# Attention and two feed-forward layers on one core: the table of attention's steps in a new order

## The chip, the core and the metric

One core of a Trainium2 chip runs the whole program: one launch, inputs and outputs in HBM. The time is device microseconds of one execution, the median of the runs shown. The engines are TensorE (PE, with its weight loads apart as PEld), VectorE (DVE), ScalarE (ACT), GpSimd (POOL) and SyncE (SP), which here only issues DMAs. Each engine works through its own instructions in the order in which they were written; a wait on a semaphore holds up all that stands behind it on that engine.

## The reference

Rotary embedding, softmax attention, then two feed-forward layers, all in float32:

```python
q_rot, k_rot = rotate(q), rotate(k)              # q, k, v: 4 x 8 x 576 x 64
scores = np.matmul(q_rot, k_rot.transpose(0, 1, 3, 2)) / np.sqrt(64)
attn = np.exp(scores - scores.max(-1, keepdims=True))
attn = attn / (attn.sum(-1, keepdims=True) + 1e-9)
x = np.matmul(attn, v)                           # to 2304 x 512
h = x @ w_in;  x = (h - np.tanh(h)) @ w_out      # 512 -> 2048 -> 512
h = x @ w_in2; x = (h / (1 + np.exp(-h))) @ w_out2
```

The weights come as 64-bit floats, and the kernel takes them apart into 32-bit ones itself, by integer operations.

## The kernel before, in words

Attention works on 16 pairs of heads, `i` = 0 to 15. The 576 positions of a head are 4 tiles of 128 and a rest of 64; a pair has 9 tiles of scores: tile 0 is head 0's first, tile 1 head 1's first and so on to tile 7, and tile 8 is the rests of both heads. Matmuls of q and k take each number as a high part and a low part (the difference), so kh, kl and qs hold both.

What a pair needs is cut into 118 steps, each on one engine. Their names, with a tile or part number behind them:

- LQ, LV, LC: loads of q and k, of v, and of a piece of weights (SP). RPnm: rotation of part n, operation m, on POOL (L310, L316, L320): n is 0 and 1 for the two heads of q, 2 and 3 for those of k, 4 for the rest rows of both. QT: PE turns the rotated tile; QE, QL: ACT's high part (L362) and DVE's low part (L367); QS0, QS1: POOL copies k's high part to the other half of the partitions (L372). QT2, QE2, QL2, QS2 do the same for the rest rows (L378 and L380 on ACT, L386 and L390 on DVE, L396 on POOL).
- S: scores on PE (L408, L409; tile 8 L415). M: row maximum on DVE (L421). E: exponential with the sum on ACT (L429). T, V: PE turns p (L465), ACT copies it out of PSUM (L474, L476). R, VR: the same for p's rest columns, copied by DVE (L443, L454, L457).
- P0x, P1x: p times v on PE (L487), for the first 256 positions and for the other 320. XC: DVE copies the result (L492). RRa, RRb, TR, RC: the reciprocals of the sums, on DVE (L510, L513), turned by PE (L517), copied by ACT (L521). RW: SP writes them to HBM (L525, L526); RS: SP reads them back, each head's over 64 partitions (L531). XN: POOL scales x by them (L497). XO: SP stores x (L504, L506).
- CM, C0 to C3, CH, CL: taking one piece of weights apart, on ACT (L122), DVE (L133, L136, L139, L142), ACT (L158) and POOL (L162).

The order is a table written by hand, ORDER_A. A step's place `x` in it and its shift `st` (the number behind + or -) give it the time `x + 118 * (i + st)`; all steps of all pairs are sorted by that, and each engine gets its own in this order. So one turn of the table, a period, holds for instance S0 of pair i, the rotation of pairs i+1 and i+2 and the scaling of pair i-2 or i-3. WARP presses the steps of later pairs that would come before or early in pair 0's time into its first 0.6 period.

Three PSUM buffers (`tp`) serve all turned tiles in the order of QT, T, R and TR, two serve the scores, one the product x. In SBUF, `xs` (x before it is scaled) has two buffers and `rs` (the reciprocals read back) one. SP's one queue carries every load and store.

Ahead of the table, from L547 on, stand pair 0's loads and its rotation, shared between DVE and POOL, with ACT, PE and DVE making the first high and low parts; `second` does head 1's before S1. Behind the last exponential the remaining steps are laid between the first matmuls of the first feed-forward layer (`head`, `own`, `on_tail`). Then come the layers, 160 blocks of 12 + 12 matmuls, in which the rest of the weights is taken apart.

Of the kernel before, what the change touches and what calls it, by code (L numbers as in the profile page):

```python
# [8 lines left out]
F32 = mybir.dt.float32  # L9
# [4 lines left out]
ACTF = mybir.ActivationFunctionType  # L14
# [15 lines left out]
def kernel(  # L30
# [188 lines left out]
    NTI = len(tiles)  # L219
    TPB = 3  # L220
    Q0 = 256
    WARP = (0.1, 0.6)
    ORDER_A = [(w.split("+")[0].split("-")[0], int(w[len(w.split("+")[0].split("-")[0]):] or 0)) for w in """
    S0 C1 CH+2 T7+1 V7+1 VR3+1 M0 XO0+3 RRa+1 T6+1 S1 M1 T8+1 R4+1 XC0+2 E0 S2 RP20-1 V6+1 V8+1 QT0-1 VR4+1 RP42-1
    RP21-1 T0 E1 RRb+1 QE00-1 TR+1 RP22-1 S3 P10+1 C2 QE01-1 RP30-1 LV P11+1 XN0+2 P12+1 RC+1 RP31-1 V0 CL+2
    QL00-1 P13+1 RP00-2 M2 RP01-2 E2 QL01-1 P14+1 RP32-1 M3 E3 XO1+2 RP10-2 RP11-2 RW+1 T1 S4 XC1+1 R0 V1 VR0 M4
    QT1-1 LC-1 S5 QE11-1 QT2-1 M5 RP40-2 P00+1 LQ-3 P01+1 QE10-1 P02+1 RS+1 T2 E4 QE2-1 E5 XN1+1 QL11-1 QL10-1 S6
    T3 QS2-1 QS1-1 QL2-1 RP12-2 M6 V2 R1 S7 V3 RP02-2 QS0-1 T4 R2 VR1 T5 C3 E6 CM-1 M7 V4 C0-1 S8 VR2 M8 P03+1
    RP41-2 E7 V5 E8 P04+1 R3
    """.split()]  # L230

    def attention(conv, on_rope_done, on_scores_near, on_scores_done):
# [22 lines left out]
        def load_qk(i):  # L255
            b, c = divmod(i, NPAIR)
            hs = slice(2 * c, 2 * c + 2)
            xm = [rp.tile([128, 2, NJ * D], F32, tag=f"xm{n}", name=f"xm{n}", bufs=2) for n in range(2)]
            xr = rp.tile([128, 2, D], F32, tag="xr", name="xr", bufs=2)
            for n, src in ((0, q), (1, k)) if i else ((1, k), (0, q)):  # L260
                nc.sync.dma_start(
                    out=xm[n],
                    in_=src[b, hs, 0:MAIN, :].rearrange("h (p j) d -> p h (j d)", j=NJ),
                )
            if i == 0:
                nc.sync.dma_start(out=csr, in_=cs_rem)
# [20 lines left out]
        def rope_ops(i, n, eng):  # L287
            st = {}

            def begin():  # L290
                rot = rot_t.setdefault(i, {})
                xm, xr = raw_t[i]
                u = n // 2
                if (i, u) == (0, 1):
                    rot[u] = None
                elif u not in rot:
                    rot[u] = (rp.tile([128, NJ, 2, D], F32, tag=f"a{u}", name=f"a{u}", bufs=1) if u < 2 else
                              rp.tile([128, 2, D], F32, tag="ar", name="ar", bufs=1))
# [65 lines left out]
        def qk_low(i, u, h):  # L364
            qs, kh, kl, qr = qk_t[i]
            c, a = main_cols(u, h), HV[h]
            DVE.tensor_tensor(out=kl[a, c] if u else qs[HV[1 - h], c], in0=tq_t[i, u][a],  # L367
                              in1=(kh if u else qs)[a, c].bitcast(F32), op=ALU.subtract)
# [119 lines left out]

        def x_copy(i, e):
            w = S - Q0 if e else Q0  # L490
            xs = xs_t[i, e] = ap.tile([128, S - Q0], F32, tag="xs", name="xs", bufs=2)
            DVE.tensor_copy(out=xs[:, 0:w], in_=x_t.pop((i, e))[:, 0:w])  # L492

        def x_norm(i, e):
# [31 lines left out]
            nc.sync.dma_start(out=rd[i][:, MAIN:S], in_=rc[NTI - 1:NTI])  # L526

        def recip_read(i):
            rs = rs_t[i] = ap.tile([128, S], F32, tag="rs", name="rs", bufs=1)
            for h in range(2):  # L530
                nc.sync.dma_start(out=rs[HV[h]], in_=rd[i][h:h + 1].to_broadcast([64, S]))  # L531

# [13 lines left out]

        nc.sync.dma_start(out=csk, in_=cs_main)  # L547
        load_qk(0)
        DVE.memset(zero, 0.0)
        for vr in vr2:  # L550
            DVE.memset(vr, 0.0)
# [6 lines left out]
            ACT.activation(out=qr[:, 0, 64:128], in_=zero, func=ACTF.Copy)  # L558
            ACT.activation(out=qr[:, 1, 0:64], in_=zero, func=ACTF.Copy)
        ACT.activation(out=csq, in_=csk, func=ACTF.Copy, scale=scale)  # L560
        for n, eng in ((2, DVE), (0, POOL), (1, DVE), (4, DVE), (3, POOL)):
            if n == 4:
                DVE.tensor_scalar(out=csr[0:64], in0=csr[0:64], scalar1=scale, scalar2=None, op0=ALU.mult)
            for f in rope_ops(0, n, eng):
                f()
        qk_alloc(0)
        kh = qk_t[0][1]

        def k_first(h):
            ACT.activation(out=k0[h][:, :, 1, :], in_=k0[h][:, :, 0, :], func=ACTF.Copy)  # L570
            tq_t[0, 1] = tp = turn(k0[h])
            ACT.activation(out=kh[:, main_cols(1, h)], in_=tp, func=ACTF.Copy)

        k_first(0)
        qk_turn(0, 0)
        qk_high(0, 0, 0)
        qk_low(0, 1, 0)
        qk_turn(0, 2)
        rest_high(0)
        qk_low(0, 0, 0)  # L580
        rest_low(0)
        rest_swap(0, DVE)

        def second():
            qk_high(0, 0, 1)
            k_first(1)
            qk_low(0, 0, 1)
            qk_low(0, 1, 1)

        before = {("S1", 0): second}  # L590
        skip = {("LQ", 0), ("LQ", 1), ("LV", 0), ("LC", 0), ("LC", 1)}
        conv.load(2)
        load_qk(1)
        END = NP - 1
        seq = [(x + len(ORDER_A) * (i + st), w, i) for x, (w, st) in enumerate(ORDER_A) for i in range(NP)]
        lead = min(t for t, w, i in seq if i and w[0] in "QR" and w[:2] != "RR")
# [305 lines left out]
```

## Time and profile before

| | |
|---|---|
| median of 3 runs | 1126.44 us (1126.17 to 1129.02) |
| the profiled execution | 1127.76 us; its span 1125.9 us |
| PE busy | 1079.5 us, 96% |
| PEld | 887.9 us, 79% |
| DVE | 800.3 us, 71% |
| ACT | 655.5 us, 58% |
| POOL | 309.4 us, 27% |
| chain that ended last | PE 75%, POOL 7%, DVE 6%, ACT 5%, DMA 3% |
| PE busy from 450 to 800 us | 348.68 of 350 us |

Busy shares are over the whole span. Attention fills the first 305 to 325 us and keeps four engines at work; the layers behind it keep PE busy and leave the others time. A change in attention is therefore read from windows inside it: here from one first row maximum (M0) to another. A row of such windows has the stretch, its length, the busy time of PE, PEld, DVE, ACT and POOL, each with its instructions in brackets, then the mean granted clock of PE as a share of 2.4 GHz, the share of DMA and its GB/s.

### The profile page before, as it was taken

What the parts mean: (1) busy time and instruction counts of PE and PEld (TensorE: products, weight loads), DVE (VectorE), ACT (ScalarE), POOL (GpSimd) and SP (SyncE); (2) the same over time, 40 slices, a digit from 0 to 9 for tenths busy, and PEclk for the clock granted to TensorE, in tenths of its full rate; (3) what the DMA queues carried; (4) which work ended last, traced back from release to release, by engine and by line L of the source; (5) the groups of instructions that cost most, each with busy time, mean ns of one, the idle gap of its engine ahead of it and who ended that gap; (6) DMA issues with size and microseconds to landing.
All of it is one profiled execution on the core that took longest, in us unless ns stands there. A gap on an engine that the chain in (4) does not pass through costs nothing.

```text
span 1125.9 us, 16650 instructions
## 1 busy us (share of the span) xinstructions
PE 1079.5 (96%) x5860; PEld 887.9 (79%) x5860; DVE 800.3 (71%) x1379; ACT 655.5 (58%) x1382; POOL 309.4 (27%) x393
## 2 busy tenths in 40 slices
PE   5898989999999999999999999999999999999998
PEld 3676767777768889888888898888888888888887
DVE  7888887788858987988999979876544533323323
ACT  4888887788967757776766657544343323222221
POOL 6687878688620101111012001111100000000000
PEclk9999999999999999999999999999999999999999
DMA  5233332423331222321333332432232203122012
GB/s 154 69 107 106 94 114 83 128 89 107 124 98 43 94 75 98 109 94 56 113 130 97 129 113 94 142 120 94 75 112 77 75 1 112 38 75 94 35 41 75
DMA packets 72402, 103.71 MB, mean 92 GB/s; under 512 B 14592, under 2 KB 51200, under 8 KB 70528
## 3 DMA queue, kind: packets, MB, share of 16 engines
q1 hardware_dynamic: 72160, 102.40, 27.8%
q8 instruction: 46, 0.75, 0.3%
q14 instruction: 36, 0.29, 0.1%
q10 hardware_dynamic: 160, 0.26, 0.1%
HBM read 78.97 MB, written 23.67 MB: 91 GB/s over the span
## 4 chain that ended last, share of the span: by engine, by line
PE 75%; POOL 7%; DVE 6%; ACT 5%; DMA 3%; issue 2%; SPq 2%; POOLq 0%; DVEq 0%; ACTq 0%
PE acc L762 35%; PE hp L686 34%; ACT p L429 2%; DMA rs<-rd 2%; DVE st L421 2%; PE x L487 2%; POOL a L320 2%; POOL kh L372 2%; PE sc L408 1%; PE tpp L465 1%; POOL xs L497 1%; POOL bm L316 1%; PE sc L409 1%; POOL kh L396 1%; ACT pt L474 1%
## 5 line engine op out<-in xcount | busy, mean ns | idle before, releaser
L686 PE MATMUL hp<-xh,win 128*128 128x512 f32 (+1 forms) x1280 | 387.6, 368 | 0.0
L697 ACT ACTIVATE t<-hp 128x512 f32<-128x512 f32 (+1 forms) x160 | 88.9, 556 | 392.7 <-PE hp L686 385.1
L731 DVE TENSOR_TENSOR gl<-t,gh 128x512 fp32r<-128x512 f32 (+1 forms) x160 | 110.5, 691 | 241.0 <-ACT gh L729 240.8
L686 PEld LDWEIGHTS hp<-xh,win 128*128 128x128 f32 x1280 | 234.3, 188 | 41.5 <-issue 0.9
L686 PE MATMUL hp<-xl,win 128*128 128x512 f32 (+1 forms) x640 | 235.5, 368 | 0.0
L762 PE MATMUL acc<-gh,wout 128*128 128x512 f32 (+1 forms) x640 | 193.8, 368 | 1.3 <-DVE xo L772 1.3
L762 PE MATMUL acc<-wout,gh 128*128 128x512 f32 x576 | 177.7, 390 | 0.0
L686 PEld LDWEIGHTS hp<-xl,win 128*128 128x128 f32 x640 | 120.7, 189 | 20.5
L762 PEld LDWEIGHTS acc<-gh,wout 128*128 128x128 f32 x640 | 117.2, 189 | 21.7 <-ACT u L701 1.7
L421 DVE TENSOR_REDUCE st<-sc 128x1 f32<-128x576 f32 x144 | 108.2, 754 | 25.9 <-PE sc L409 21.2
L429 ACT ACTIVATE p<-sc,st 128x576 f32<-128x576 f32 x144 | 106.5, 740 | 31.9 <-DVE st L421 29.7
L762 PEld LDWEIGHTS acc<-wout,gh 128*128 128x128 f32 x576 | 107.1, 188 | 21.3
L762 PE MATMUL acc<-gl,wout 128*128 128x512 f32 (+1 forms) x320 | 117.8, 368 | 0.0
L162 POOL TENSOR_TENSOR wout<-wa,wout 128x512 fp32r<-128x512 f32 x32 | 46.6, 1458 | 242.6 <-ACT wout L158 229.1
L162 POOL TENSOR_TENSOR win<-wa,win 128x512 fp32r<-128x512 f32 x32 | 42.8, 1339 | 256.0 <-ACT win L158 256.0
L762 PE MATMUL acc<-wout,gl 128*128 128x512 f32 x288 | 112.0, 389 | 0.0
L408 PE MATMUL sc<-kh,qs 128*128 128x288 f32 x256 | 86.1, 351 | 18.3 <-POOL kh L372 13.6
L729 ACT ACTIVATE gh<-t 128x512 fp32r<-128x512 f32 (+1 forms) x160 | 93.7, 585 | 1.4 <-PE acc L762 1.4
L465 PE MATMUL tpp<-ident,p 128*128 128x128 f32 x576 | 87.2, 281 | 2.1 <-ACT pt L474 1.1
L474 ACT ACTIVATE pt<-tpp 128x512 f32<-128x512 f32 x128 | 73.6, 589 | 18.7 <-PE tpp L465 18.7
L465 PEld LDWEIGHTS tpp<-ident,p 128*128 128x128 f32 x576 | 68.6, 144 | 16.1 <-ACT p L429 7.3
L409 PE MATMUL sc<-kl,qs 128*128 128x288 f32 x256 | 74.3, 304 | 0.1
(103 smaller groups left out, 1776.7 us busy)
## 6 DMA issues: line engine op xcount, KB each, us to landing
raw<-in_moe_w_in_dram SPq DMA_DIRECT2D x32, 512.0 KB
raw<-in_moe_w_out_dram SPq DMA_DIRECT2D x32, 512.0 KB
xin<-xd SPq DMA_DIRECT2D x14, 1024.0 KB
pd<-xo SPq DMA_DIRECT2D x34, 256.0 KB
xo<-pd SPq DMA_DIRECT2D x34, 256.0 KB
rs<-rd SPq DMA_DIRECT2D x32, 144.0 KB
xm<-in_k_dram SPq DMA_DIRECT2D x16, 256.0 KB
xm<-in_q_dram SPq DMA_DIRECT2D x16, 256.0 KB
```

Source lines behind the costliest of these rows:

```text
L162: POOL.tensor_tensor(out=w[:, 1], in0=self.val.pop(j), in1=w[:, 0].bitcast(F32), op=ALU.subtract)
L408: PE.matmul(sc[:, e, 0:HALF], lhsT=l, rhs=kh[:, c], start=True, stop=False)
L409: PE.matmul(sc[:, e, 0:HALF], lhsT=l, rhs=kl[:, c], start=False, stop=True)
L421: DVE.tensor_reduce(out=st, in_=s_t[i, n][:, :, 0:HALF], op=ALU.max, axis=AX.XY, negate=True)
L429: ACT.activation(out=p_t[i, j][:, h % 2].rearrange("p (e s) -> p e s", e=2), in_=s_t.pop((i, n))[:, :, 0:HALF], func=ACTF.Exp, bias=st_t.p ...
L465: PE.transpose(tp[:, cc * 128:(cc + 1) * 128], p[:, p0 + cc * 128:p0 + (cc + 1) * 128], ident)
L474: ACT.activation(out=t[0][:, :, h, o:o + 128], in_=tp.rearrange("p (c s) -> p c s", c=NJ), func=ACTF.Copy)
L686: PE.matmul(hp, lhsT=w[:, a, ws], rhs=bb, start=(n == 0), stop=(n == 3 * KD - 1))
L697: ACT.activation(out=t, in_=hp, func=ACTF.Tanh, scale=0.5 if l else 1.0)
L729: ACT.activation(out=gh, in_=t, func=ACTF.Copy)
L731: DVE.tensor_tensor(out=gl, in0=t, in1=gh.bitcast(F32), op=ALU.subtract)
L762: PE.matmul(acc, lhsT=a, rhs=bb, start=(fi == 0 and n == 0), stop=(fi == NH - 1 and n == 2))
```

## The change

Four things: (1) the table has a new order and new shifts, and WARP starts 0.12 period earlier; (2) `xs` has three buffers and `rs` two; (3) pair 1's loads of q and k are issued right behind pair 0's, ahead of v's and the weights'; (4) pair 0's first rotation is shared anew: DVE takes parts 2, 0 and 3, POOL parts 1 and 4 (before: DVE 2, 1 and 4, POOL 0 and 3), part 3's three operations are laid between DVE's low parts, ACT scales the table of the rest rows, and ACT writes the rest rows of k to both places out of PSUM, so that DVE's copies (L396) go. Of the table, whose rows tell nothing by themselves, two lines stand here.

```diff
-    WARP = (0.1, 0.6)
+    WARP = (-0.02, 0.6)
...
-    S0 C1 CH+2 T7+1 V7+1 VR3+1 M0 XO0+3 RRa+1 T6+1 S1 M1 T8+1 R4+1 XC0+2 E0 S2 RP20-1 V6+1 V8+1 QT0-1 VR4+1 RP42-1
...
+    S0 RP12-1 RW+2 M0 LQ-2 LV+1 RRa+1 RP31-1 T7+1 V7+1 E0 C2 P03+2 P04+2 XC0+2 T8+1 S1 M1 R4+1 RP32-1 XN0+3 S2
+    V8+1 VR4+1 QT1-1 T0 E1 RS+2 QT0-1 XN1+2 S3 P10+1 C0-1 QE10-1 M2 P11+1 RP41-1 RRb+1 QE11-1 P12+1 C3 QL10-1
...
-            xs = xs_t[i, e] = ap.tile([128, S - Q0], F32, tag="xs", name="xs", bufs=2)
+            xs = xs_t[i, e] = ap.tile([128, S - Q0], F32, tag="xs", name="xs", bufs=3)
...
-            rs = rs_t[i] = ap.tile([128, S], F32, tag="rs", name="rs", bufs=1)
+            rs = rs_t[i] = ap.tile([128, S], F32, tag="rs", name="rs", bufs=2)
...
         load_qk(0)
+        load_qk(1)
...
-        for n, eng in ((2, DVE), (0, POOL), (1, DVE), (4, DVE), (3, POOL)):
-            if n == 4:
-                DVE.tensor_scalar(out=csr[0:64], in0=csr[0:64], scalar1=scale, scalar2=None, op0=ALU.mult)
-            for f in rope_ops(0, n, eng):
-                f()
...
+        first = {n: rope_ops(0, n, eng) for n, eng in ((2, DVE), (0, DVE), (1, POOL), (4, POOL), (3, DVE))}
...
+        for f in first[2]:
+            f()
+        k_dup(0)
+        ACT.activation(out=csr[0:64], in_=csr[0:64], func=ACTF.Copy, scale=scale)
+        for n in (0, 1, 4):
+            for f in first[n]:
+                f()
+        k_turn(0)
+        qk_low(0, 1, 0)
+        first[3][0]()
         qk_turn(0, 0)
         qk_high(0, 0, 0)
-        qk_low(0, 1, 0)
+        first[3][1]()
+        qk_low(0, 0, 0)
         qk_turn(0, 2)
-        rest_high(0)
-        qk_low(0, 0, 0)
+        for h in range(2):
+            for o in rest_cols(kh, h):
+                ACT.activation(out=o, in_=rest_of(tq_t[0, 2], h), func=ACTF.Copy)
+        for h in range(2):
+            ACT.activation(out=qr[HV[h], h, 64 * h:64 * h + 64], in_=tq_t[0, 2][HV[h], 0:64], func=ACTF.Copy)
+        first[3][2]()
         rest_low(0)
-        rest_swap(0, DVE)
...
         conv.load(2)
-        load_qk(1)
```

What the new table does to the engines' orders, at three places in the middle of attention. First POOL, around one period's scaling (xs<-xs,rs) and its copies of k (CAST kh<-kh; 64x64 and 64x2x64 are the rest rows, 64x512 is a head). Before:

```order
L310 TENSOR_TENSOR ar<-xr,csr 128x128
L497 TENSOR_TENSOR xs<-xs,rs 128x320
L396 CAST kh<-kh 64x64
L396 CAST kh<-kh 64x2x64
L372 CAST kh<-kh 64x512
L320 TENSOR_TENSOR a_1411<-a_1411,bm 128x4x64 x2
L372 CAST kh<-kh 64x512
L316 TENSOR_TENSOR br<-xr,csr 128x128
```

And now:

```order
L310 TENSOR_TENSOR ar<-xr,csr 128x128
L396 CAST kh<-kh 64x64
L396 CAST kh<-kh 64x2x64
L310 TENSOR_TENSOR a_1449<-xm_1316,csk 128x4x64
L320 TENSOR_TENSOR a_1449<-a_1449,bm 128x4x64
L320 TENSOR_TENSOR a_1430<-a_1430,bm 128x4x64
L316 TENSOR_TENSOR bm<-xm_1316,csk 128x256
L320 TENSOR_TENSOR a_1449<-a_1449,bm 128x4x64
L497 TENSOR_TENSOR xs<-xs,rs 128x256
L497 TENSOR_TENSOR xs<-xs,rs 128x320
L316 TENSOR_TENSOR br<-xr,csr 128x128
L372 CAST kh<-kh 64x512
```

Before, the scaling of 320 columns stood directly ahead of all copies of k; now the rest rows' copies are ahead of both scalings, and the scalings ahead of one head's copy.

Second DVE, from M0 on (TENSOR_REDUCE st<-sc is a row maximum, wa a step of the weights, qs and kl low parts). Before:

```order
L421 TENSOR_REDUCE st<-sc 128x1
L510 TENSOR_SCALAR rr<-sums 128x9
L421 TENSOR_REDUCE st<-sc 128x1
L492 COPY xs<-x 128x256
L457 COPY pr_2129<-tpt 64x64 x2
L513 RECIPROCAL rr<-rr 128x9
L139 SCALAR_TENSOR_TENSOR wa<-raw,wa 128x512
L367 TENSOR_TENSOR qs<-tpq,qs 64x512
L421 TENSOR_REDUCE st<-sc 128x1
```

And now:

```order
L421 TENSOR_REDUCE st<-sc 128x1
L510 TENSOR_SCALAR rr<-sums 128x9
L139 SCALAR_TENSOR_TENSOR wa<-raw,wa 128x512
L492 COPY xs<-x 128x256
L421 TENSOR_REDUCE st<-sc 128x1
L457 COPY pr_2085<-tpt 64x64 x2
L133 TENSOR_SCALAR wa<-raw 128x512
L421 TENSOR_REDUCE st<-sc 128x1
L513 RECIPROCAL rr<-rr 128x9
L142 SCALAR_TENSOR_TENSOR wa<-wm,wa 128x512
L367 TENSOR_TENSOR kl_145<-tpq,kh 64x512 x2
L367 TENSOR_TENSOR qs<-tpq,qs 64x512
```

Three steps of the weights, where there was one, and k's low parts now stand among the first row maxima.

Third SP, from the write of the reciprocals (rd<-rc) to their read (rs<-rd). Before:

```order
L525 DMA rd_88<-rc 4x2x128
L526 DMA rd_88<-rc 2x1x64
L112 DMA raw<-in_moe_w_in_dram 128x4x256
L261 DMA xm_1475<-in_q_dram 128x2x256
L261 DMA xm_1476<-in_k_dram 128x2x256
L268 DMA xr<-in_q_dram 64x2x64
L268 DMA xr<-in_k_dram 64x2x64
L531 DMA rs<-rd_88 64x576 x2
```

And now:

```order
L525 DMA rd_88<-rc 4x2x128
L526 DMA rd_88<-rc 2x1x64
L261 DMA xm_1595<-in_q_dram 128x2x256
L261 DMA xm_1596<-in_k_dram 128x2x256
L268 DMA xr<-in_q_dram 64x2x64
L268 DMA xr<-in_k_dram 64x2x64
L279 DMA vm<-in_v_dram 128x2x256
L284 DMA vr_142<-in_v_dram 64x64 x2
L531 DMA rs<-rd_88 64x576 x2
L112 DMA raw<-in_moe_w_in_dram 128x4x256
```

The load of v has come between write and read, and the load of weights has gone behind the read.

## Rows read from the trace of the kernel before

**Rows 1.** Busy time by windows, each from one M0 to a later one.

```profile
15.11:55.05 39.94, 33.53 (x216) 26.22 (x215) 32.73 (x59) 31.07 (x73) 29.11 (x45) 1.00 0.23 67
55.05:269.48 214.43, 195.17 (x1455) 152.46 (x1453) 180.07 (x341) 176.15 (x418) 169.63 (x243) 0.98 0.34 104
74.10:169.85 95.75, 87.48 (x663) 67.87 (x661) 82.78 (x156) 79.94 (x190) 76.94 (x111) 1.00 0.35 107
169.85:231.52 61.67, 55.18 (x398) 43.85 (x397) 48.08 (x94) 48.38 (x114) 46.43 (x67) 0.94 0.32 98
269.48:305.20 35.72, 34.47 (x267) 27.02 (x265) 32.18 (x62) 31.61 (x76) 25.32 (x36) 1.00 0.38 118
```

**Rows 2.** Chain of waits, one period: start us, us, engine, tile, line.

```profile
130.53 0.40 PE sc L408
...
131.45 0.76 DVE st L421
...
141.23 3.03 DMA rs<-rd
...
144.42 0.88 POOL xs L497
```

**Rows 3.** Timeline of SP's queue, the same period.

```profile
128.82 0.37 SPq L279 DMA_DIRECT2D vm<-in_v_dram  x1
...
129.29 1.11 SPq L284 DMA_DIRECT2D vr<-in_v_dram  x2
...
136.23 0.69 SPq L525 DMA_DIRECT2D rd<-rc  x1
```

**Rows 4.** Table of waits, 103 to 255 us: total, times, longest.

```profile
POOL xs L497 <- DMA rs<-rd: 17.7, 5, 4.1
```

**Rows 5.** Busy time by windows, 190 to 195 us.

```profile
190.00:195.00 5.00, 5.00 (x31) 4.92 (x30) 3.52 (x8) 3.82 (x8) 4.51 (x7) 0.66 0.00 0
```

**Rows 6.** Timeline of PE, first scores of one pair.

```profile
188.94 0.40 PE L408 MATMUL sc<-kh,qs 128*128 128x288 f32 x1 [1.87 <-POOL kh L372]
```

**Rows 7.** Groups by line, 112.26 to 169.85 us (three periods).

```profile
L421 DVE TENSOR_REDUCE st<-sc 128x1 f32<-128x576 f32 x28 | 21.1, 754 | 5.3 <-PE sc L409 4.9
...
L429 ACT ACTIVATE p<-sc,st 128x576 f32<-128x576 f32 x27 | 20.0, 740 | 5.7 <-DVE st L421 5.3
...
L454 DVE COPY pr<-tpt 128x128 f32<-128x128 f32 x12 | 3.4, 284 | 1.5 <-PE tpt L443 1.5
...
L142 DVE SCALAR_TENSOR_TENSOR wa<-wm,wa 128x512 f32<-128x512 f32 x3 | 2.8, 941 | 0.1
...
L122 ACT ACTIVATE wm<-raw 128x512 f32<-128x512 f32 x3 | 2.0, 675 | 0.0
...
L474 ACT ACTIVATE pt<-tpp 128x512 f32<-128x512 f32 x24 | 13.8, 589 | 3.5 <-PE tpp L465 3.5
```

**Rows 8.** Timeline of ACT and DVE, parts of the rest rows.

```profile
122.92 0.50 ACT L378 ACTIVATE kh<-tpq 64x64 fp32r<-64x64 f32 x2
...
123.45 0.45 ACT L380 ACTIVATE qr<-tpq 64x64 fp32r<-64x64 f32 x2
...
123.93 0.53 DVE L386 TENSOR_TENSOR kl<-tpq,kh 64x64 fp32r<-64x64 f32 x2 [0.17 <-ACT qr L380]
...
124.47 0.46 DVE L390 TENSOR_TENSOR qr<-tpq,qr 64x64 fp32r<-64x64 f32 x2
```

**Rows 9.** Timeline of DVE, pair 0's preparation.

```profile
4.64 0.42 DVE L316 TENSOR_TENSOR bm<-xm,csk 128x256 f32<-128x256 f32 x1
...
6.04 0.95 DVE L316 TENSOR_TENSOR bm<-xm,csq 128x256 f32<-128x256 f32 x1
...
11.44 0.68 DVE L367 TENSOR_TENSOR qs<-tpq,qs 64x512 fp32r<-64x512 f32 x1
...
13.39 1.43 DVE L396 CAST kh<-kh 64x64 fp32r<-64x64 f32 x2
```

**Rows 10.** Timeline of DVE, a conversion step with POOL idle.

```profile
320.01 0.68 DVE L142 SCALAR_TENSOR_TENSOR wa<-wm,wa 128x512 f32<-128x512 f32 x1
```

More of the change, by code (lines that the diff above doesn't have):

```diff
@@ L221 @@
     Q0 = 256
-    WARP = (0.1, 0.6)
+    WARP = (-0.02, 0.6)
     ORDER_A = [(w.split("+")[0].split("-")[0], int(w[len(w.split("+")[0].split("-")[0]):] or 0)) for w in """
-    S0 C1 CH+2 T7+1 V7+1 VR3+1 M0 XO0+3 RRa+1 T6+1 S1 M1 T8+1 R4+1 XC0+2 E0 S2 RP20-1 V6+1 V8+1 QT0-1 VR4+1 RP42-1
[L225 to L229, printed above, removed]
+    S0 RP12-1 RW+2 M0 LQ-2 LV+1 RRa+1 RP31-1 T7+1 V7+1 E0 C2 P03+2 P04+2 XC0+2 T8+1 S1 M1 R4+1 RP32-1 XN0+3 S2
+    V8+1 VR4+1 QT1-1 T0 E1 RS+2 QT0-1 XN1+2 S3 P10+1 C0-1 QE10-1 M2 P11+1 RP41-1 RRb+1 QE11-1 P12+1 C3 QL10-1
+    QL11-1 LC-2 P13+1 QE00-1 V0 QL00-1 P14+1 QS1-1 M3 E2 RP00-2 QE01-1 XO0+3 R0 S4 RP10-2 QL01-1 RP11-2 RP01-2 VR0
+    RP20-2 CH T1 TR+1 RP42-1 E3 M4 QS0-1 RP02-2 C1-1 T3 V1 S5 T2 E4 RC+1 XC1+1 M5 S6 R1 V3 P00+1 V2 P01+1 E5 P02+1
+    M6 RP21-2 E6 R2 CM-2 QT2-1 QE2-1 VR1 VR2 S7 T4 S8 M7 CL QL2-1 T6 V4 T5 M8 RP40-2 E7 QS2-1 RP30-2 RP22-2 R3 V6
+    XO1+2 V5 E8 VR3
     """.split()]
@@ L560, in attention, with k_dup, k_turn @@
         ACT.activation(out=csq, in_=csk, func=ACTF.Copy, scale=scale)
-        for n, eng in ((2, DVE), (0, POOL), (1, DVE), (4, DVE), (3, POOL)):
-            if n == 4:
-                DVE.tensor_scalar(out=csr[0:64], in0=csr[0:64], scalar1=scale, scalar2=None, op0=ALU.mult)
-            for f in rope_ops(0, n, eng):
-                f()
         qk_alloc(0)
-        kh = qk_t[0][1]
-        def k_first(h):
+        kh, qr = qk_t[0][1], qk_t[0][3]
+        first = {n: rope_ops(0, n, eng) for n, eng in ((2, DVE), (0, DVE), (1, POOL), (4, POOL), (3, DVE))}
+        def k_dup(h):
             ACT.activation(out=k0[h][:, :, 1, :], in_=k0[h][:, :, 0, :], func=ACTF.Copy)
+        def k_turn(h):
             tq_t[0, 1] = tp = turn(k0[h])
             ACT.activation(out=kh[:, main_cols(1, h)], in_=tp, func=ACTF.Copy)
-        k_first(0)
+        for f in first[2]:
[8 more added lines that the diff above has]
+        first[3][0]()
         qk_turn(0, 0)
         qk_high(0, 0, 0)
-        qk_low(0, 1, 0)
+        first[3][1]()
+        qk_low(0, 0, 0)
         qk_turn(0, 2)
-        rest_high(0)
-        qk_low(0, 0, 0)
+        for h in range(2):
[4 more added lines that the diff above has]
+        first[3][2]()
         rest_low(0)
-        rest_swap(0, DVE)
         def second():
             qk_high(0, 0, 1)
-            k_first(1)
+            k_dup(1)
+            k_turn(1)
             qk_low(0, 0, 1)
```

## The prediction, made before the change was run

> **What bounds the kernel now.** The page's slices show TensorE (PE) short of full only in the first third; from about 325 us on, in the two matmul layers, it hardly stops, and the change touches nothing there. So the end moves by what attention, before it, loses or gains. I read attention by the row maximum of the first tile of each pair of heads, which I call M0: it starts at 15.11 us for pair 0 and at 305.20 us for pair 15, so 15 periods take 290.1 us, 19.34 us on average. The windows between M0s [rows 1] give the parts. Pairs 3 to 8 take 95.75 / 5 = 19.15 us each at full clock; in one such period PE is busy 17.5 us, VectorE (DVE) 16.56, ScalarE (ACT) 15.99, GpSimd (POOL) 15.39. Nobody is full, so a wait sets the period. Pairs 8 to 11 take 61.67 / 3 = 20.56 us with a mean granted clock of 0.94. The last two take 17.86 us each: there are no more loads of q and k, and the same order, DVE as busy per period as before (16.1 us), runs 1.3 us faster.
>
> The chain of waits names the wait [rows 2]. The read-back of the reciprocals (rs<-rd) is in flight 3.03 us; POOL's scaling of x stands waiting for it, and only then come POOL's copies of k, the first score matmul at 130.53 in the period shown, M0 at 131.45, and through DVE the sums of the next reciprocals. The loop closes through SP's queue: their write is issued at 136.23, the read lands at 144.26, 8.03 us later [rows 2, 3]. The table of waits gives POOL's wait for that read 17.7 us in 152 us [rows 4]. What a longer stop costs besides: at 188.94 us the first scores have waited 1.87 us for the late copy of k, and in the 5 us from 190 on the granted clock is 0.66, that is, most of that stretch at 1.2 GHz in place of 2.4 [rows 5, 6]. The three periods around it cost 61.67 - 3 x 19.15 = 4.2 us over the others.
>
> **The change, part by part.**
>
> *Read-back and scaling.* Counted in periods of the table from a pair's own S0, the scaling of the first block (XN0) goes from 2.31 to 3.17 and that of the second (XN1) from 1.69 to 2.25; the second rs buffer and the third xs buffer carry the longer lives. ACT's copy of the reciprocals (RC) goes from 1.33 to 1.65, so from it to XN1 the table now has 0.60 period, 11 us at 18.3, where before it had 0.36, 6.9 us, less than the 8.03 it needs. In SP's queue one load of the conversion leaves the way, which I don't credit, and the load of v, three issues, 0.37 + 1.11 us, joins it [rows 3]: 8.03 + 1.5 = 9.5 us. The write waits on SP for RC, and behind it stand the loads of q, k and v, the read, the next weight and the two stores of x. All of them have half a period or more before anyone needs them, so this wait is covered. If it runs out, XN1 is late and with it POOL's two copies of k behind it; POOL has 2 to 3 us of its own slack per period (18.3 less 15.4) for that. The 3 us wait goes away; what is late next?
>
> *The new loop.* I follow the new order from the first scores S0. The first matmul to M0: 131.45 - 130.53 = 0.92 us [rows 2]. Then DVE has twenty steps from M0 to M5, the six row maxima among them, without one that must wait: what each needs is ready earlier, most tightly the second low part of q, whose ACT copy is done about 1 us ahead. DVE's whole period is 16.56 us [rows 1]; outside that run lie three row maxima (0.754 each), three copies of turned p (0.284 each) and the low parts of the rest rows (0.53 + 0.46) [rows 7, 8]: 16.56 - 2.26 - 0.85 - 0.99 = 12.46 us. Behind M5 ACT has, in one piece, two exponentials (0.740 each), the magnitude (0.675), four copies of the rest rows (0.50 + 0.45), one copy of turned p (0.589) and the exponential E7 (0.740) [rows 7, 8]: 4.44 us. PE's turn R3 and with it the next S0 stand behind E7. Handing over, four times about 0.1 us, and R3 itself: 0.5 us. Sum: 0.92 + 12.46 + 4.44 + 0.5 = **18.3 us**.
>
> POOL must deliver the copy of the rest rows before that S0. Its own work is 15.39 us per period, and it waits once, for ACT's copy of k before QS1: it ends about 1 us ahead. So the period is 18.3 us, set by DVE and ACT, and PE no longer has a stop of 1.9 us in it. I take it that the clock stays up.
>
> *Periods.* Eleven from 55.05 to 269.48: 11 x 18.3 = 201.3 for 214.43: -13.1 us, 4.2 of them the clock's. The last two: 36.6 for 35.72, +0.9, since the new loop is not one that the loads shorten. The first two: the second gains as the others, -0.9; the first is left as it is, since it still has the second half of pair 0's preparation in it.
>
> *The first rotation.* Before, the low part of q is ready at 12.12, but the second half of the first scores waits for DVE's two copies of the rest rows, 1.43 us to 14.82 [rows 9]. They go: ACT writes both places from PSUM, two more small copies. The rotation of the rest rows and the scaling of their table leave DVE, one rotation of q comes to it; q is turned as early as now, since DVE and POOL still do one head each. I put DVE's low part of q near 11 us, the rest rows' low part near 12.4, and M0 near 13.1: -2.0 us. Bounds: 0, if POOL's rest rows come as late as DVE's did, and -2.5. The loads of pair 1 come ahead of those of v and of the weights; what POOL waits for them now lies beside pair 0's work, so I count nothing.
>
> *The tail.* Steps of the last pairs change places, but PE has matmuls of the first layer to do from 325 us on, and the new order leaves POOL and SP alone with the later scalings: 0. If a scaling were late, the first block of the layer that needs it is the third.
>
> **A rule against it.** DVE instructions with two operands in SBUF get longer beside POOL: the same product takes 0.42 us alone and 0.95 beside POOL [rows 9], the last conversion step 0.68 alone and 0.941 in the mean [rows 7, 10]. POOL now works 15.4 of 18.3 us, 84%, where it worked 80% of 19.15: by these rows three such steps per period lose 0.05 us together. The Trainium skill, SBUF — State Buffer (Who interferes with whom), calls the port pair of the two engines an exclusive lock: the one that comes second is blocked for the other's whole instruction, which would charge a whole POOL instruction each time. By that the sum would be the slower rival below; the trace agrees on the direction alone.
>
> **The sum.** -2.0 - 0.9 - 13.1 + 0.9 = -15.1 us. The profiled execution took 1127.76 us (span 1125.9 and 1.9 around it), 1.3 us over the median of the runs: 1127.76 - 15.1 = **1112.7 us**.
>
> Bounds of the period: below 17.2 us no row shows PE's work done (34.47 / 2 in the last two [rows 1]); above, nothing is gained but the clock, 19.0. I take 18.3 since it comes from the order itself.
>
> **The rivals.**
> - *PE becomes the bound.* The estimate of the run on DVE takes busy time as if nothing overlapped with the next wait. If the handshakes close up better, the period nears PE's 17.2 and a handover, 17.3: 14 periods x 1.0 us more (all but the first), 1112.7 - 14 = about 1099. For it: PE is busy 17.2 of 17.86 in the last two periods. Against: DVE is nearly as full, and the run from M0 to M5 has no gap to close.
> - *Another wait takes the place.* The read lands later than XN1 by more than POOL's slack, or POOL's copy of the rest rows, which now stands just ahead of S0, is late. The period is then near that of before at full clock, 19.0: -2.0 for the start, 209.0 - 214.4 = -5.4, +2.3 in the last two, -0.2: 1122.5 us. For it: the rest rows' turn, copies and POOL copy moved into the last fifth of the period, and three loads joined the queue ahead of the read. Against: 9.5 us stand against 11.
> - *Slower: DVE blocked by POOL.* In the new order three conversion steps with two SBUF operands lie in the one run that sets the period, two of them between row maxima that ACT waits for. If each waits for a whole POOL instruction (about 0.73 us, in place of the 0.26 that 0.941 - 0.68 shows), 3 x 0.47 = 1.4 us join the period: 19.7 us, 15 x 19.7 - 290.1 = +5.4, and the start -2.0 gives 1131 us. It decides from 1.2 us per period on: 19.47 x 15 = 292.1, which is what the start gives back. This is what the Trainium skill's rule, SBUF — State Buffer (Who interferes with whom), would make of it. Against: these steps run beside a POOL that is 80% busy already.
>
> **How the numbers follow.** The forecast gets 0.60, PE as the bound 0.17, another wait 0.15, the blocked DVE 0.08. A measurement of this kernel can tell 0.3%, 3.4 us, from no change: faster is below 1123.1, slower above 1129.8. The forecast and the first rival lie below; of the second rival, at 1122.5, two thirds: faster 0.87, same 0.05, slower 0.08. The forecast's own range, 0.35 us a period either way, is 1107 to 1118; to hold 8 in 10 it reaches to the first rival and over the second: **1099 to 1124 us**.
>
> **What would show it.** Right: windows between M0s of 18.0 to 18.6 us in the middle, at a granted clock of 1.00; POOL's xs no longer waiting for rs<-rd; the chain going through DVE from M0 to M5, ACT from E5 to E7, and PE; the first M0 near 13.1 us. Wrong: a row in which POOL waits for rs<-rd or DVE, PE for kh on POOL for more than a few tenths per period; the conversion steps on DVE at 1.3 us or more; clock windows below 0.9; or a period under 17.6 us.

## The result, and the profile after

| | before | after |
|---|---|---|
| median, lowest to highest (4 runs each) | 1127.45 us, 1126.17 to 1129.02 | **1111.30 us**, 1110.27 to 1112.32 |
| the profiled execution, its span | 1127.76, 1125.9 us | 1111.48, 1109.7 us |
| chain that ended last | PE 75%, POOL 7%, DVE 6%, ACT 5%, DMA 3% | PE 86%, DVE 7%, ACT 5%, DMA and POOL 0% |

The ratio is 0.9856, with a 95% interval of 0.9838 to 0.9874: 1.4% faster. The predicted 1112.7 us is 1.4 us above, and the range holds the time. From here on the text asks whether the reasons were right, too.

The page's busy times and its chain by engine, after:

```profile
PE 1076.4 (97%) x5860; PEld 885.4 (80%) x5860; DVE 789.4 (71%) x1376; ACT 654.9 (59%) x1385; POOL 308.7 (28%) x393
...
PE 86%; DVE 7%; ACT 5%; issue 1%; DMA 0%; POOL 0%; SPq 0%; DVEq 0%; POOLq 0%; ACTq 0%
```

DMA and POOL have left the chain. ACT is as busy as before, PE 3 us less; DVE is 11 us less busy, which I hadn't forecast and which comes up again below.

Busy time by windows, after, from one M0 to a later one, cut as in [rows 1] (stretch, length, busy PE, PEld, DVE, ACT, POOL, granted clock, DMA share, GB/s):

```profile
13.62:56.60 42.98, 34.41 (x211) 28.17 (x212) 31.68 (x59) 32.93 (x77) 31.10 (x48) 0.92 0.23 70
56.60:254.00 197.40, 190.62 (x1454) 148.33 (x1453) 174.88 (x342) 174.82 (x420) 170.29 (x242) 1.00 0.37 112
254.00:289.12 35.12, 34.30 (x266) 26.96 (x265) 30.93 (x62) 31.43 (x77) 23.55 (x34) 1.00 0.37 120
```

Against [rows 1] this settles the sum by its terms:

| term | before | after | measured | predicted |
|---|---|---|---|---|
| start, to the first M0 | 15.11 | 13.62 | -1.5 | -2.0 |
| first two periods | 39.94 | 42.98 | **+3.0** | -0.9 |
| eleven periods | 214.43 | 197.40 | **-17.0** | -13.1 |
| last two periods | 35.72 | 35.12 | -0.6 | +0.9 |
| from the last M0 to the end | 820.70 | 820.58 | -0.1 | 0 |
| sum | 1125.9 | 1109.7 | -16.2 | -15.1 |

The eleven periods now take 17.95 us each, not 18.3, and PE is busy 190.62 / 11 = 17.33 us of each. The mean granted clock is 1.00 over the eleven periods, where before it was 0.98 [rows 1], with the 5 us of [rows 5] at 0.66. The first two periods lost 3 us, at a mean clock of 0.92 for 1.00. Two errors of 3.9 us, one each way, cancel in the predicted total: that it came within 1.4 us is luck.

The table of waits after, 103 to 255 us, has this row in the place of [rows 4] (total, times, longest):

```profile
POOL xs L497 <- DMA rs<-rd: 2.5, 5, 0.7
```

17.7 us of waiting have become 2.5, and no row in it has PE waiting for POOL's kh any more, as in [rows 6]. The 17.7 us are the five waits that end with the read; before's table has three more of the same scaling, put down to other engines:

```profile
POOL xs L497 <- ACT pt L474: 6.7, 2, 3.6
...
POOL xs L497 <- DVE qr L390: 2.9, 1, 2.9
```

The scaling uses neither of these results, so it was most likely the read here too: 27.3 us in eight waits, 3.4 us per period. SP's write of the reciprocals and one period's scalings on POOL's timeline, after:

```profile
140.41 0.69 SPq L525 DMA_DIRECT2D rd<-rc  x1
...
148.14 1.27 POOL L497 TENSOR_TENSOR xs<-xs,rs 128x256 f32<-128x256 f32 x1
149.81 0.86 POOL L497 TENSOR_TENSOR xs<-xs,rs 128x320 f32<-128x320 f32 x1 [0.40 <-DMA rs<-rd]
```

The second scaling still stands 0.40 us for the read. From the write's issue to its start are 149.81 - 140.41 = 9.4 us, so the round trip takes what I put, 9.5; but POOL comes to it after 9.0 us, and the 11 us that I read off the table's places were not there. It doesn't matter as long as POOL has slack; how much it has is the sixth experiment.

What sets the period now? The same period (M0 at 146.84, the next at 164.52), cut at the end of M5; windows as above:

```profile
146.84:159.10 12.26, 11.90 (x91) 8.90 (x91) 11.71 (x22) 10.69 (x25) 10.62 (x15) 1.00 0.30 94
159.10:164.52 5.42, 5.42 (x45) 4.60 (x42) 3.94 (x11) 5.22 (x15) 4.80 (x9) 1.00 0.53 162
```

DVE's run from M0 to M5 takes 12.26 us (predicted 12.46), and the rest 5.42 (predicted 0.92 + 4.44 + 0.5 = 5.86). But in the second part PE is busy for all of 5.42 us, and in the first for 11.90 of 12.26. So the loop that I counted is there in its length, but PE has nearly no hole beside it. The chain of this stretch, after, doesn't go the way that I put as a sign of being right (DVE from M0 to M5, ACT from E5 to E7): from 156.66 to 167.1 it lies on PE alone (start us, us, engine, tile, line):

```profile
156.66 0.66 PE tpp L465 x4
...
158.94 1.45 PE x L487 x12
...
163.65 0.27 PE tpt L443
163.93 0.14 PE sc L408
...
164.35 0.14 PE sc L409
...
164.92 1.01 PE x L487 x8
...
168.89 0.76 DVE st L421
...
169.77 0.55 DVE wa L142
...
171.65 0.70 DVE qs L367
...
172.37 0.59 ACT qs L362
```

Then it crosses to DVE (the row maximum M2, a conversion step, low parts) and ACT (q's copy, a conversion step, an exponential) and returns to PE. No DMA and no POOL are in it. The lines from 163.65 on are R3 and the next S0, whose four matmuls take from 163.93 to 164.49, 0.56 us.

### The profile page after: what moved, and what is told of

Same layout as the page of the kernel before. It is cut to its first block, busy times and chain, and to the rows that moved or that the text cites. A ratio compares the mean times of both kernels' runs of the same rounds, so it can differ in the third digit from the quotient of the medians.

```text
span 1109.7 us, 16730 instructions
## 1 busy us (share of the span) xinstructions
PE 1076.4 (97%) x5860; PEld 885.4 (80%) x5860; DVE 789.4 (71%) x1376; ACT 654.9 (59%) x1385; POOL 308.7 (28%) x393
## 4 chain that ended last, share of the span: by engine, by line
PE 86%; DVE 7%; ACT 5%; issue 1%; DMA 0%; POOL 0%; SPq 0%; DVEq 0%; POOLq 0%; ACTq 0%
PE acc L774 35%; PE hp L698 35%; PE tpp L465 5%; PE x L487 4%; PE sc L409 2%; PE sc L408 2%; ACT p L429 2%; DVE kl L367 2%; DVE st L421 2%; PE sc L415 1%; DVE qs L367 1%; ACT qs L362 1%; PE tpt L443 1%; DVE wa L142 1%; PE tpq L336 1%
```

## The experiments

All times are medians; each ratio is against the kernel before on the same chip, with its 95% interval. Against such intervals (about 2 us either way) differences between the faster kernels of 1 to 2 us are not certain; where they matter, the M0s of the traces are given too.

**1. The later scalings alone, in the table of before.** All else is as before: order, shifts, start.

```diff
-    S0 C1 CH+2 T7+1 V7+1 VR3+1 M0 XO0+3 RRa+1 T6+1 S1 M1 T8+1 R4+1 XC0+2 E0 S2 RP20-1 ...
+    S0 C1 CH+2 T7+1 V7+1 VR3+1 M0 RRa+1 T6+1 S1 M1 T8+1 R4+1 XC0+2 E0 S2 XN0+3 RP20-1 ...
...
-    RP21-1 T0 E1 RRb+1 QE00-1 TR+1 RP22-1 S3 P10+1 C2 QE01-1 RP30-1 LV P11+1 XN0+2 P12+1 ...
+    RP21-1 T0 E1 RRb+1 QE00-1 TR+1 RP22-1 XN1+2 S3 P10+1 C2 QE01-1 RP30-1 LV P11+1 P12+1 ...
...
-    ... M3 E3 XO1+2 RP10-2 ...
+    ... M3 E3 XO0+3 XO1+2 RP10-2 ...
...
-    ... E4 QE2-1 E5 XN1+1 QL11-1 ...
+    ... E4 QE2-1 E5 QL11-1 ...
...
-            xs = ... bufs=2)
+            xs = ... bufs=3)
-            rs = ... bufs=1)
+            rs = ... bufs=2)
```

> The kernel before with one thing of the change: XN0 and XN1 (and the stores XO behind them) stand later in its own table, with rs in two buffers and xs in three; order, rotation and loads otherwise as before. If the wait for the read-back alone held the period: POOL's wait for rs<-rd goes, the eleven periods after the second fall from 19.5 to what the old table's last two take, 17.9 us, no clock window under 0.9: 197 for 214.4 us, about 1111 us. If the gain is the new order of the other steps: the periods stay at 18.7 to 19.1, only the clock's 4 us come back: 1121 to 1124 us.

Measured: 1109.68 us, ratio 0.984 (0.982 to 0.986). The windows from M0 to M0:

```profile
14.94:53.39 38.45, 32.44 (x216) 25.42 (x215) 32.17 (x59) 30.62 (x73) 29.76 (x46) 1.00 0.21 62
53.39:251.13 197.74, 190.68 (x1455) 148.52 (x1453) 179.43 (x342) 175.11 (x419) 170.68 (x243) 1.00 0.37 112
251.13:287.05 35.92, 34.67 (x266) 27.00 (x265) 32.52 (x63) 31.97 (x78) 24.55 (x35) 1.00 0.41 124
```

Eleven periods of 17.98 us, as in the whole change, and a clock of 1.00. This is all of the gain, and the first two periods lose nothing (38.45 us). The rest of the new table, which I had followed step by step to get 18.3, brings nothing to the period beyond this.

**2. The change with the start of before.** Loads of pair 1 and first rotation as they were.

```diff
-        load_qk(1)
-        first = {n: rope_ops(0, n, eng) for n, eng in ((2, DVE), (0, DVE), (1, POOL), (4, POOL), (3, DVE))}
...
+        for n, eng in ((2, DVE), (0, POOL), (1, DVE), (4, DVE), (3, POOL)):
...
         conv.load(2)
+        load_qk(1)
```

> The changed kernel with the preamble of before (first rotation, order of the first loads, DVE's copies of the rest rows); the table stays new. If the new start is worth what the first M0 shows: M0 back from 13.6 to 15.1 us and the time up by 1.5 us, 1112.8. If the time lost in the first two periods (42.98 us against 39.94) comes from the new start: it falls back, and the time is 1.5 us lower, 1109.8. If that loss comes from the table (pair 0's second half of the preparation written behind E0): 1112 to 1113 with the long gap between M0 and M1 of pair 0 still there (6 us).

Measured: 1113.57 us, 0.9876 (0.9855 to 0.9897), 2.3 us more than the change. M0 of pair 0 is at 14.69 us (13.62 in the change) and of pair 2 at 57.68 (56.60). The start is worth 1.1 us in the trace. This trace's eleven periods are 1.8 us longer, too (199.00 us, where the change has 197.22, cut as in the fifth run); why, is open. The second row maximum still comes 6.4 us behind the first (14.69, 21.06), so the loss of the first periods does not come from the new start.

**3. Before, with the new start.** The reverse of the second.

> The kernel before with the new preamble alone; its table puts the second half of pair 0's preparation ahead of E0. If the new start is a gain by itself: M0 at 13.6 us, the gap to M1 as before, 3.4 us, and 1.5 us less, about 1126 us. If the loads of v and weights, now behind pair 1's, or the new sharing cost as much later: M0 of pair 2 at 55 us as before and no change, 1127.5 us.

Measured: 1127.66 us, 0.9997 (0.9984 to 1.0010). M0 of pair 0 comes at 13.19 us and of pair 2 at 53.85, 1.9 and 1.2 us earlier than before. In the time nothing of it can be seen, where 1126 was expected: the runs lie from 1124.91 to 1130.35. Inconclusive on its own; the eighth run repeats it where the loop is steady. One M0 alone doesn't settle the start either: over the traces of this record it comes at 14.33 to 15.11 us in the four kernels with the old start, and at 13.19 to 13.70 in the seven with the new one that do all of the scores' work.

**4. The second half of pair 0 ahead of E0.** In the change the table has the exponential E0 ahead of S1; before it was behind. The preparation of pair 0's second half (`second`) hangs on S1, so all its ACT work stands behind E0 in ACT's order, and E0 waits for M0. ACT's timeline after:

```profile
14.41 0.74 ACT L429 ACTIVATE p<-sc,st 128x576 f32<-128x576 f32 x1 [1.87 <-DVE st L421]
15.25 0.59 ACT L362 ACTIVATE qs<-tpq 64x512 fp32r<-64x512 f32 x1
15.87 0.42 ACT L567 ACTIVATE k<-k 128x256 f32<-128x256 f32 x1
...
17.49 0.60 ACT L571 ACTIVATE kh<-tpq 128x512 fp32r<-128x512 f32 x1 [1.21 <-PE tpq L336]
```

ACT stands 1.87 us for M0, and k's copy (L567) is behind that; PE waits for it, and the second row maximum comes at 20.00, 6.4 us after the first, where before it was 3.4 (15.11 and 18.50). The edit moves the hook:

```diff
-        before = {("S1", 0): second}
+        before = {("E0", 0): second}
```

> The changed kernel with one thing more: the second half of pair 0's preparation is written ahead of E0 in place of ahead of S1. If ACT's queue, with E0 ahead of the copies of k, makes the 6.4 us between M0 and M1 of pair 0: that gap shrinks to about 4 us and the time falls by 2 to 2.5 us, to about 1109. If the first two periods are held by the rotation of pair 1 on POOL or by the clock: M0 of pair 1 stays at 39.5 us and the time at 1111.

Measured: 1109.99 us, 0.9842 (0.9823 to 0.9862). ACT's copy and DVE's second row maximum on the timeline:

```profile
12.92 0.42 ACT L567 ACTIVATE k<-k 128x256 f32<-128x256 f32 x1
...
17.05 0.76 DVE L421 TENSOR_REDUCE st<-sc 128x1 f32<-128x576 f32 x1 [1.18 <-PE sc L409]
```

k's copy is 2.95 us earlier, and the second row maximum comes 3.6 us behind M0 again. M0 of pair 2 is at 53.93 in place of 56.60: 2.7 us come back at that point, 1.3 us in the median. So the cause of most of the +3.0 is shown: the preparation's copies on ACT put behind an exponential that waits. Its own first two periods still take 40.44 us, with M0 of pair 0 at 13.49; the mean granted clock in them is 0.92, as in the change, where before it was 1.00. PE's timeline and a 5 us window show a stop of PE and a low clock behind it, as in [rows 5, 6]:

```profile
27.45 1.11 PE L465 MATMUL tpp<-ident,p 128*128 128x128 f32 x4 [1.89 <-DVE st L421]
```

```profile
28.00:33.00 5.00, 4.76 (x26) 4.28 (x24) 2.41 (x6) 3.27 (x9) 3.94 (x5) 0.62 0.00 0
```

That the stop is what lowers it, no run tried.

**5. PE's work made less.** The products with k's low part are left out in eight of the nine score tiles. If PE sets the period, it follows; if the loop through DVE and ACT does, it stays.

```diff
-                    PE.matmul(sc[:, e, 0:HALF], lhsT=l, rhs=kh[:, c], start=True, stop=False)
-                    PE.matmul(sc[:, e, 0:HALF], lhsT=l, rhs=kl[:, c], start=False, stop=True)
+                    PE.matmul(sc[:, e, 0:HALF], lhsT=l, rhs=kh[:, c], start=True, stop=True)
```

> The changed kernel without the products of q with k's low part in tiles 0 to 7 (its scores are less exact); PE has 16 matmuls fewer per period, 16 x 0.13 = 2.1 us, the other engines' work is the same. If PE's own work sets the 17.94 us: the period falls to about 16 us, where DVE and ACT (15.8 and 15.9 busy) hold it, 30 us less in all, about 1082. If the run on DVE and ACT sets it, as predicted: only the part of S0 ahead of M0 shortens, 0.3 us, some more where row maxima wait for scores, 17.2 to 17.7 us, 1100 to 1107 us.

Measured: 1106.56 us, 0.9807 (0.9790 to 0.9823). Eleven periods, from one step on the sums (rr) to another, of the change and of this kernel:

```profile
61.63:258.85 197.22, 190.44 (x1453) 148.27 (x1452) 174.70 (x343) 174.65 (x419) 170.66 (x241) 1.00 0.37 112
```

```profile
58.99:253.49 194.50, 177.28 (x1276) 125.96 (x1274) 174.39 (x342) 173.97 (x418) 171.15 (x241) 0.99 0.38 113
```

PE's busy time falls by 13.16 / 11 = 1.2 us per period (2.1 were expected), the period only from 17.93 to 17.68 us. So PE's own work is not what sets it: a loop of 17.68 us stands in which PE has room. In the chain of 150 to 190 us of this kernel the row maxima on DVE have 17.4% and the exponentials on ACT 12.9%. It is the loop of the prediction from M2 to E7; ahead of M2 it lies in part on PE. Its way through ACT from E5 to E7, R3 and S0, in another period:

```profile
120.11 0.82 ACT p L428 x2
120.94 0.57 ACT wm L122
...
123.00 0.73 ACT p L428 x2
...
123.78 0.33 PE tpt L442
124.11 0.27 PE sc L408 x2
```

But the edit shortens this loop, too: S0 has two matmuls here, 0.27 us where the change has 0.56. That 0.29 us alone would make the quarter of a microsecond, so the run doesn't show whether PE, full beside the loop, adds anything to it. A difference of this size is also hardly above the scatter of such readings: by the same steps, the four kernels with the new order and all of PE's work have periods of 17.83 (fourth run), 17.93 (the change), 18.01 (seventh) and 18.09 us (second).

**6. The change with one rs buffer.** The read of the reciprocals must then wait until the scalings of the pair before have let the buffer go. This takes POOL's slack away and measures it.

```diff
-            rs = ... bufs=2)
+            rs = ... bufs=1)
```

> The changed kernel with rs in one buffer: the read-back of a pair may start only when XN0 of the pair before is done, just ahead of XN1 on POOL, so POOL waits for a transfer of about 3 us in each period. If POOL has the 2 to 3 us of slack that the prediction gives it: the period grows by 0.5 to 1 us, 1119 to 1126 us. If POOL has none: by the whole 3 us, 20.9 us, about 1155. If the wait costs nothing: 1111.

Measured: 1133.55 us, 1.0045 (1.0030 to 1.0061): slower than before. The table of waits, 103 to 255 us, and eleven periods:

```profile
POOL xs L497 <- DMA rs<-rd: 35.0, 8, 4.7
```

```profile
61.54:279.69 218.15, 193.46 (x1448) 147.85 (x1447) 170.12 (x342) 178.53 (x418) 167.69 (x242) 1.00 0.33 98
```

POOL waits 35.0 / 8 = 4.4 us per period, and the period grows to 218.15 / 11 = 19.83, by 1.9 us. So POOL's slack in the change is about 4.4 - 1.9 = 2.5 us; the prediction had put it at 2 to 3. The slack was right, but a wait of 3 us was expected, and so the time came out above the 1126. It is also the rival "another wait" in the flesh: POOL stands for the read again. In the new order the second buffer carries the gain.

**7. DVE's run shortened in front.** The addition of 1e-9 to the sums, 0.44 us on DVE between M0 and M1 (L510), is left out.

```diff
-            DVE.tensor_scalar(out=r_t[i][:, 0], in0=sum_t.pop(i), scalar1=1e-9, scalar2=None, op0=ALU.add)
...
-            DVE.reciprocal(out=r_t[i][:, 1], in_=r_t[i][:, 0])
+            DVE.reciprocal(out=r_t[i][:, 1], in_=sum_t.pop(i))
```

> The changed kernel without RRa: the 1e-9 added to the sums is left out (a sum is at least 1, so nothing of it is left in float32), 0.44 us less on DVE between M0 and M1 of each period. If DVE's run from M0 to M5 sets the period: 15 x 0.3 to 0.44, 4.5 to 6.6 us less, 1105 to 1107. If PE's work sets it: no change, 1111.

Measured: 1110.39 us, 0.9838 (0.9821 to 0.9854), and eleven periods:

```profile
60.93:259.04 198.11, 190.40 (x1453) 148.20 (x1452) 174.76 (x331) 174.71 (x419) 169.62 (x241) 1.00 0.38 112
```

18.01 us per period: no shorter. The row has DVE as busy as in the change (174.70) with a dozen instructions fewer. The conversion step that now follows M0 (L139) grew from 0.68 to 0.97 us in the mean. So this edit did not take work from DVE's run, and it can't tell whether that run's front is on the loop; it shows that taking one step away can lengthen another. The tenth run asks again where the work does go.

**8. The first experiment with the new start.**

> The kernel before with the late scaling (e1) and the new preamble (e3), so all of the change but the new order. If the gains add: e1's periods of 17.96 us from pair 2 on and e3's M0 of pair 2 at 53.9 in place of 55.05, but e1's own stood at 53.4: 0.5 to 1.5 us less than e1, 1108 to 1109. If the new start's gain is lost in the first two periods, as in the changed kernel: 1110.

Measured: **1108.56 us**, 0.9823 (0.9808 to 0.9837), the lowest median of the kernels here that leave out no work, though its interval overlaps those of the first and the ninth run. The second period's step on the sums (the reciprocal, L513) comes at 54.91 us, 1.3 us earlier than in the first experiment, with the same periods of 17.97; the median is 1.1 us lower. With the second run this puts the new start at 1.1 to 1.3 us where the loop behind it is steady.

**9. The second scaling alone.** In the table of before only XN1 moves, from 1.69 to 2.25 periods, with its store XO1 right behind it. XN0 stays, rs keeps one buffer and xs two.

```diff
-    RP21-1 T0 E1 RRb+1 QE00-1 TR+1 RP22-1 S3 ...
+    RP21-1 T0 E1 RRb+1 QE00-1 TR+1 RP22-1 XN1+2 XO1+2 S3 ...
...
-    ... M3 E3 XO1+2 RP10-2 ...
+    ... M3 E3 RP10-2 ...
...
-    ... E4 QE2-1 E5 XN1+1 QL11-1 ...
+    ... E4 QE2-1 E5 QL11-1 ...
```

> The kernel before with XN1 alone moved, from 1.69 to 2.25 periods, its store right behind it; XN0 stays, rs keeps one buffer and xs two. If the place of XN1 against the read-back is all that held the period: periods of 18.0 us as in e1, 1110 us. If the third xs buffer or the second rs buffer is needed for it: DVE's copy of x waits for a store, or SP's read-back for XN0, and the periods stay above 18.5, 1117 us or more.

Measured: 1109.78 us, 0.9838 (0.9821 to 0.9854). Eleven periods, and the waits that lead the table of 103 to 255 us:

```profile
56.41:254.18 197.77, 190.72 (x1453) 148.40 (x1452) 177.79 (x341) 175.13 (x419) 170.29 (x243) 1.00 0.37 113
```

```profile
ACT p L429 <- DVE st L421: 14.0, 25, 0.8
...
POOL xs L497 <- DVE xs L492: 4.8, 9, 0.5
```

17.98 us per period, and no wait for the read. One step moved out from ahead of k's copies on POOL, 3 lines of a table, gives all that the large change gives. In this order, where XN0 keeps its place, one rs buffer and two of xs are enough; the change, with its later XN0, needs the second rs buffer (sixth run). Its third xs buffer was not tried alone.

**10. The eighth without the addition of 1e-9.** The seventh again, in the old order.

> e8 (late scaling and new preamble in the old table) without the 1e-9, as in e7. If a loop through DVE between M0 and M1 holds e8's 17.96 us: up to 6 us less, 1102. If, as its chain shows, ACT and PE hold it: as e8 within 1 us, 1108.

Measured: 1108.64 us, 0.983 (0.9816 to 0.9845), as the eighth. Eleven periods of the eighth and of this one, each from one reciprocal to a later one:

```profile
54.91:252.60 197.69, 190.71 (x1455) 148.59 (x1453) 180.43 (x341) 175.48 (x419) 170.35 (x242) 1.00 0.36 112
```

```profile
56.01:253.57 197.56, 190.71 (x1454) 148.52 (x1453) 173.90 (x331) 175.20 (x419) 170.16 (x242) 1.00 0.36 112
```

Here the work does leave DVE, (180.43 - 173.90) / 11 = 0.59 us per period, and the periods don't move: 17.97 and 17.96 us. In this order what DVE does just behind M0 is not on the loop.

## Why the prediction was right, and where it wasn't

*The wait that goes.* Right, and shown. POOL's wait for the read-back ahead of k's copies closed the loop: with the scalings alone moved (first run), or XN1 alone (ninth), the period goes to 17.98 us; with the wait put back (sixth), it rises to 19.83. If the three waits put down to other engines are the read's, too, it cost POOL 3.4 us in each of the eight periods, and [rows 4] shows two thirds of it.

*The clock.* Right for the eleven periods, wrong for the first two (0.92, where they had 1.00). In [rows 5] the clock fell to 0.66 behind a stop of PE; of the kernels with the wait taken out, none has a clock under 0.99 over its eleven periods. The 4.2 us priced for it are an estimate within the 17.0, not measured apart. That the stop was what took the clock away is seen in the traces, not tried by itself. It isn't POOL's wait as such: in the sixth run POOL waits longer than before, PE's longest wait in those periods is 1.6 us where it was 1.9, and the clock is 1.00.

*The new loop, 18.3 us.* The mechanism was right as far as the fifth run goes, the size off by 0.35 us per period, eleven times: 3.9 us. The step that failed is that of pricing the run from M0 to M5 by DVE's busy time before, with nothing waiting: in the period shown it has 11.71 us of work and 0.55 of gaps, where I had 12.46 and none. The rest took 5.42 us for 5.86: ACT's piece from E5 to E7 4.24 us for 4.44, R3, S0 and the hand-overs 1.18 for 1.42. What I did not see is that PE is full beside it: 17.32 of the 17.68 us of that period, and the chain lies on PE for 10.4 us at a stretch. The mean period is also just under the 18.0 to 18.6 us that I gave as a sign of being right. The rival "PE becomes the bound" gave 17.3 us, and the middle periods lie between that and my forecast. The fifth run speaks against it: 1.2 us less on PE gave 0.25, no more than S0's own shortening. With S0 in full its loop would be 17.68 + 0.29 = 17.97 us, an estimate, and that is the period already. So the loop through DVE and ACT is enough to explain the period; that PE adds to it is not shown, and not excluded.

*DVE's busy time, and the rule against the change.* The forecast took before's 16.56 us of DVE per period, and the slower rival let it grow. It fell, to 174.88 / 11 = 15.90. Groups by line (xcount, then busy us, mean ns, idle before), three periods of before, DVE and then POOL:

```profile
L139 DVE SCALAR_TENSOR_TENSOR wa<-raw,wa 128x512 int32<-128x512 int32 x3 | 3.5, 1156 | 0.0
L136 DVE SCALAR_TENSOR_TENSOR wa<-raw,wa 128x512 int32<-128x512 int32 x3 | 2.9, 982 | 0.0
...
L510 DVE TENSOR_SCALAR rr<-sums 128x9 f32<-128x9 f32 x3 | 2.2, 726 | 0.0
...
L316 POOL TENSOR_TENSOR bm<-xm,csk 128x256 f32<-128x256 f32 x6 | 5.8, 960 | 0.0
...
L497 POOL TENSOR_TENSOR xs<-xs,rs 128x256 f32<-128x256 f32 x3 | 2.2, 733 | 0.0
```

and of after:

```profile
L136 DVE SCALAR_TENSOR_TENSOR wa<-raw,wa 128x512 int32<-128x512 int32 x3 | 3.3, 1116 | 0.1
L139 DVE SCALAR_TENSOR_TENSOR wa<-raw,wa 128x512 int32<-128x512 int32 x3 | 2.0, 680 | 0.0
L142 DVE SCALAR_TENSOR_TENSOR wa<-wm,wa 128x512 f32<-128x512 f32 x3 | 1.9, 630 | 0.0
...
L510 DVE TENSOR_SCALAR rr<-sums 128x9 f32<-128x9 f32 x3 | 1.3, 442 | 0.1
...
L316 POOL TENSOR_TENSOR bm<-xm,csk 128x256 f32<-128x256 f32 x6 | 4.4, 727 | 0.0
...
L497 POOL TENSOR_TENSOR xs<-xs,rs 128x256 f32<-128x256 f32 x3 | 3.3, 1088 | 0.0
```

The same instructions changed length: L139 from 1156 to 680 ns, L142 from the 941 of [rows 7] to 630, the 9 columns of L510 from 726 to 442; L136 grew from 982 to 1116. On POOL the scaling of 256 columns went from 733 to 1088, the product bm with k's table from 960 to 727. So lengths changed both ways on both engines, and what DVE lost did not go over to POOL: over the eleven periods DVE has 174.88 us for 180.07, POOL 170.29 for 169.63 [rows 1]. The Trainium skill, SBUF — State Buffer (Who interferes with whom), says that of a DVE instruction with two SBUF inputs and a GpSimd instruction that reads SBUF, whichever issues first holds the shared port pair for its whole instruction and the other blocks until then. None of the extra lengths here, 0.48 us at most, is a whole neighbour of 0.7 us; the rule allows that where the second comes late, so a whole instruction each time, as the forecast's rival had it and always at DVE's cost, is its upper end. That the neighbour is the cause is read from the lengths alone; no run tested it. Nor is it where the gain came from: in the eighth run DVE is about as busy as before (16.4 us per period), in the tenth 0.6 us less, and the periods of both are those of the change.

*First two periods, -0.9.* Wrong, +3.0. The sentence "the first is left as it is" failed: I looked for what the second half of pair 0 does, not for where the table hangs it. E0 now stands ahead of S1, and with it ahead of that half's copies on ACT (fourth run, which gives back 2.5 of the 3.0).

*Start, -2.0.* Nearly right, -1.5 in the trace; M0 at 13.62 where I had 13.1. The low part of q ends at 11.01 as put, the rest rows' low part of k at 13.11, not 12.4, and M0 stands behind that of q on DVE. *The last two, +0.9:* wrong in sign. The new loop is not longer than the old one without loads: 17.56 us. *The tail, 0:* right, -0.1.

*What stays open.* Why the old order and the new come out within 0.05 us of each other, is not settled. In the old order it isn't DVE's busy time (tenth run). In the new one no run took work from DVE; over the eleven periods of the four kernels named at the fifth run, 17.83 to 18.09 us, DVE is busy for 173.70, 174.70, 174.76 and 176.78 us, so there period and DVE's work rise together, as the forecast's loop would have it, but these kernels differ in more than that. PE's 17.33 us are common to both orders, but the fifth run, which takes some of them away, was made in the new order only; the old order with less work on PE was not tried.

## What to carry to other kernels

When four engines are 80 to 91% busy and none is full, look for the one wait that closes the loop from one iteration to the next, and move the single step that waits behind the work that others need; here 3 lines of a table gave what a new order with more buffers gave. After reordering a software pipeline, follow each in-order engine through the first iteration as well, where work is hung on a step by name: a step moved past its neighbour takes along whatever hangs on it. And before pricing a run of steps by their busy time, see how full the other engines are beside it, and take step lengths from the order that they will have; and when an experiment takes work from one engine, check first whether that work also stands on the loop of the rival, or it can't tell the two apart.

## What was not expected of the hardware

An elementwise instruction's length on DVE and POOL is not fixed: the same conversion step took 680 or 1156 ns in the mean, the same scaling on POOL 733 or 1088, with nothing changed but the order; what it depends on, no run isolates. Taking an instruction of 0.44 us per period from DVE left its busy time where it was in one order (seventh run, 174.70 and 174.76 us over eleven periods), as other steps grew (L139 by 0.29 us), and lowered it by 0.59 us per period in the other (tenth run).
